# A fused attention and gated MLP kernel: casts of the next pair's q and k over three blocks, later X loads, an addition on ScalarE

## The chip, the cores and the metric

The kernel runs on one core of one Trainium2 chip. The metric is the device time of one execution in microseconds. The engines are named as the profile names them: PE (TensorE), ACT (ScalarE), DVE (VectorE), POOL (GpSimd) and SP (SyncE, which here issues DMAs).

## The reference

Attention with rotary embedding over 32 heads, its output taken as 2304 rows of 512, and a gated MLP on these rows, all in float32. `rotate` multiplies the two halves of q and k by cosines and sines of the position.

```python
def _attn_ref(q, k, v):                       # 4 x 8 heads, 576 tokens, 64 wide
    q_rot, k_rot = (rotate(q), rotate(k))
    scores = scale * np.matmul(q_rot, k_rot.transpose(0, 1, 3, 2))
    scores = scores - np.max(scores, axis=-1, keepdims=True)
    attn = np.exp(scores)
    attn = attn / (np.sum(attn, axis=-1, keepdims=True) + 1e-09)
    return np.matmul(attn, v).astype(np.float32)

def _moe_ref(x, w_gate, w_val, w_out):         # 2304 x 512, 512 x 1536 (two), 1536 x 512
    g = x @ w_gate
    silu = g * (1.0 / (1.0 + np.exp(-g)))
    val = x @ w_val
    return (silu * val @ w_out).astype(np.float32)
```

## The kernel before

**Tiling.** Attention works on 16 pairs of heads. A pair has 9 blocks of scores, 128 rows by 576 columns each; block 8 is made of the last 64 rows of both heads (its tile of exps is Et). PE works with float32 numbers that are split into a high and a low part. For each block PE writes the scores into PSUM (L349, two buffers `sc`), DVE takes the maximum (L364), ACT the exp with the sum of each row (L382), PE transposes the exps (L425, three buffers `tr`), ACT casts the transposed tile to its high part (L426) and DVE takes the low part (L427). The results are ET1 for the blocks 0 to 3 and ET2 for the rest; the columns 512 to 575 of the keys go to TK1 and TK2 (L435 to L441). PE multiplies them with the split values VS (L465, groups of ten products into one buffer `pv`), ACT copies the result to Y (L470), and SP stores it to DRAM (`yd`, L484 to L490).

**Two pairs overlap.** While pair p runs its scores, the second half of the products of pair p - 1 is still under way, and pair p + 1 is prepared. Its q and k have been loaded as X (L175) two pairs earlier and rotated on POOL one pair earlier (L206 to L208). PE transposes them in pair p in three groups: the tail (L293), q and k (L289, four transposes each). ACT casts each group to its high part into the tile N (L308), DVE adds the low part (L312). When the last group is cast, `qk_stack` issues eight DMAs on SP (L319 to L326), the folds, that lay high and low parts side by side into QK, QZ and BD, which the score products read. POOL also splits the values (L278, L279), whose load VR (L186) SP issues when the split before has ended, and prepares the MLP's operands (tiles Xab and R, L644 to L647, and weights, L724 to L731).

**What sets the order.** `PLAN` says at which block of a pair each step is written into the program. The row `qk` has three cases, for pair 0, pair 1 and all later ones; each gives the block for the groups in the order of `qkw`, which is tail, q, k for the later pairs. The program's order is kept on POOL, on PE through pair 0 and on SP through block 48 (pair 5). Elsewhere a scheduler orders the instructions of each engine anew, by its own estimates, so that an edit of `PLAN` moves neighbours as well. Each engine then works strictly in its order; SP issues a DMA only when the one before it has been issued. In pairs 3, 7, 11 and 15 `rsum` takes the reciprocal of the sums of four pairs plus 1e-9 (L392, L393), and PE transposes it in the next pair (L400). Behind attention the MLP runs with products in fewer multiplications than the plain form (L842, L1472); its first weights are loaded and cut by `wfirst` (L772), for the gate and the value, in the middle of attention and, as f = 1, in the last pair.

Of the kernel before, what the change touches and what calls it, by code (L numbers as in the profile page):

```python
# [14 lines left out]
ALU = mybir.AluOpType  # L15
# [13 lines left out]
    trb=3,  # L29
    warm=[9, 0, 1, 2, 0, 1],  # L30
    order=["qk", "scores", "trans", "pv", "exp", "evac", "rstore", "rope", "tails", "conv", "x", "conv1", "vsplit"],
    qk=[[3, 4, 6], [1, 2, 3], [0, 0, 1]],
    qkw=[[0, 2, 1], [2, 0, 1], [2, 0, 1]],
    tails=[4, 0],
    pv=[1, 6, 5, 3, 7, 8, 2, 7, 3],
    pv0=[0, 0, 0, 0, 0, 0, 10, 10, 2],
    lqk=0,
    lv=4,
    rope=1,
    vsplit=8,  # L40
# [73 lines left out]
class Attn:  # L114
# [274 lines left out]
    def rsum(self, b):  # L389
        nc = self.nc  # L390
        rt = self.rr_p.tile([128, 36], FP32, name="rt")
        nc.vector.tensor_scalar(out=rt, in0=self.sumt, scalar1=1e-9, scalar2=None, op0=ALU.add)  # L392
        nc.vector.reciprocal(out=rt, in_=rt)  # L393
        self.rt = rt

# [113 lines left out]
class Moe:  # L509
# [255 lines left out]
    def wfirst(self, f, i):  # L765
        if f == 0:
            tmp = self.again(f"xa1{'hl'[i]}", [128, 1536], U32, "raw")
        else:
            tmp = self.again(f"raw{i}", [128, (1536, 1024)[i]], U32, "raw")
        if (f, i) != (1, 1):  # L770
            self.X1 = tmp[:, 1024:1536]
        self.nc.sync.dma_start(out=tmp[:, 0:1024], in_=self.wsrc(i, f))  # L772
        raw, X = tmp[:, 0:1024].rearrange("p (f t) -> p f t", t=2), self.X1
        if f == 0:
            return self.bits10(raw, X, *self.Wb[f][i])
        return self.bits9(raw, X, *self.Wb[f][i], self.nc.gpsimd)
# [154 lines left out]
def attn_swiglu(ctx: ExitStack, tc: tile.TileContext, qk, vr, wg, wv, wo, main, tail, out):  # L931
    nc = tc.nc
# [5 lines left out]
    NP = B * H // 2  # L938
# [108 lines left out]
    P, cvq, cv1 = PLAN, {}, {}  # L1047
# [5 lines left out]
    for n in range(NB):  # L1053
        p, b = divmod(n, 9)
        if n == 9:
            ctl1.__exit__(None, None, None)
        if (p, b) == (NP - 1, 0):
            assert not any(cvq.values())
            early.close()
            moe.open_early(mctx, pl)  # L1060
        if n == 48:
            ctl0.__exit__(None, None, None)
        if n == 5:
            at.load_v(1)
        if b == (2 if 1 < p < 6 else P["lqk"]) and 0 < p < NP - 3:
            at.load_qk(p + 3)
        if b == (1 if p < 6 else P["lv"]) and 0 < p < NP - 1:
            at.load_v(p + 1)
        for name in P["order"]:
            steps[name](n, p, b)  # L1070
            if name == "qk" and n == P["qk"][0][2]:
                at.load_qk(3)
        if p == NP - 1 and ynext and NP - 2 in at.done:
            moe.yload(ynext.pop(0), 0)
# [432 lines left out]
```

## Time and profile before

| | us |
|---|---|
| time, median of 3 runs | 690.63 |
| lowest and highest of the runs | 690.6, 691.76 |
| the profiled execution, its own time | 690.11 |
| span of its profile | 688.3 |
| TensorE busy | 677.4 |
| VectorE busy | 582.4 |
| ScalarE busy | 424.2 |
| GpSimd busy | 470.1 |

The table's busy times are sums over the whole span. The granted clock of TensorE is 1.00 in all the windows read here, which is the level of 2.4 GHz. Times in a timeline are counted from the start of the span. Attention takes the time from 9.3 us, with the first scores, to 273.2 us, the last ones; a pair begins with the first score product of its block 0.

### The profile page before, as it was taken

Reading aid. Unit: us, or ns where it says so; the run is one execution under the profiler, and the core shown is the slowest. Engines: PE = TensorE matmul, PEld = TensorE weight load, DVE = VectorE, ACT = ScalarE, POOL = GpSimd, SP = SyncE. Lnnn points to the kernel's source line nnn. Section 1 sums busy time; section 2 is a strip of 40 time slices with the busy share of each in tenths; the row PEclk is TensorE's granted clock in tenths of the full one; section 3 lists DMA queues with packets and bytes.
Section 4 is the critical chain, followed back from the end, with each engine's and each line's share of the span. In section 5 each row is a group of like instructions: output and inputs, shape, how many; then the busy total and the mean of one; then the engine's idle time right before and its main releaser. Section 6 shows DMA issues by size and latency. Waiting matters only on the chain. (4 is left out here: it accounts for less than half of the span.)

```text
span 688.3 us, 12675 instructions
## 1 busy us (share of the span) xinstructions
PE 677.4 (98%) x4414; PEld 664.3 (97%) x4414; DVE 582.4 (85%) x883; ACT 424.2 (62%) x873; POOL 470.1 (68%) x475
## 2 busy tenths in 40 slices
PE   7999999999999999999999999999999999999998
PEld 6899999999999999999999999999999999999997
DVE  5888898888888888979988898988999599877683
ACT  5899988888888888555543434424435375344341
POOL 8899799999999985998889588677784720000000
PEclk9999999999999999999999999999999999999999
DMA  6897999889988879791214345354464797627101
GB/s 195 185 248 205 218 225 243 208 206 243 246 206 208 220 189 285 187 235 70 90 58 164 122 141 204 130 187 150 161 212 163 264 317 252 207 74 247 47 24 69
DMA packets 78784, 125.76 MB, mean 183 GB/s; under 512 B 16880, under 2 KB 55680, under 8 KB 78720
## 3 DMA queue, kind: packets, MB, share of 16 engines
q1 hardware_dynamic: 75248, 118.77, 60.6%
q10 hardware_dynamic: 3472, 6.18, 2.4%
q8 instruction: 35, 0.57, 0.4%
q14 instruction: 29, 0.24, 0.1%
HBM read 66.91 MB, written 33.10 MB: 145 GB/s over the span
## 5 line engine op out<-in xcount | busy, mean ns | idle before, releaser
L364 DVE TENSOR_REDUCE nmt<-sc 128x1 f32<-128x576 f32 x144 | 108.2, 751 | 20.3 <-PE sc L349 18.9
L382 ACT ACTIVATE E<-sc,nmt 128x576 f32<-128x576 f32 x128 | 97.5, 761 | 1.7 <-DVE nmt L364 1.6
L425 PE MATMUL tr<-ident,E 128*128 128x128 f32 x512 | 77.1, 274 | 0.4 <-DVE ET1l L427 0.2
L425 PEld LDWEIGHTS tr<-ident,E 128*128 128x128 f32 x512 | 61.2, 141 | 3.4 <-PE tr L289 1.3
L1472 PE MATMUL ch<-dW,dO 128*128 128x384 f32 x216 | 63.8, 337 | 0.2 <-DVE dW L1420 0.2
L206 POOL TENSOR_TENSOR t<-X,tab 128x256 f32<-128x256 f32 (+2 forms) x94 | 54.4, 600 | 9.4 <-DMA X<-in_qk_dram 5.8
L349 PE MATMUL sc<-QK 128*128 128x288 f32 x240 | 58.7, 325 | 1.4 <-ACT E L382 0.6
L426 ACT CAST ET2h<-tr 128x512 fp32r<-128x512 f32 x80 | 47.2, 590 | 14.0 <-PE tr L425 13.7
L427 DVE TENSOR_TENSOR ET2l<-tr,ET2h 128x512 fp32r<-128x512 f32 x80 | 53.1, 682 | 2.1 <-ACT ET2h L426 2.0
L349 PE MATMUL sc<-N,QZ 128*128 128x288 f32 x240 | 51.3, 296 | 0.0
L695 POOL TENSOR_TENSOR W<-WF,W 128x1024 fp32r<-128x1024 f32 x20 | 48.1, 2409 | 3.8 <-ACT W L695 3.7
L208 POOL TENSOR_TENSOR rot<-rot,t 128x512 f32<-128x512 f32 (+2 forms) x47 | 47.0, 999 | 3.7
L427 DVE TENSOR_TENSOR ET1l<-tr,ET1h 128x512 fp32r<-128x512 f32 x64 | 43.0, 685 | 7.0 <-ACT ET1h L426 6.7
L207 POOL TENSOR_TENSOR rot<-X,tab 128x512 f32<-128x512 f32 (+2 forms) x47 | 47.0, 1001 | 0.0
L1472 PE MATMUL ch<-dH,dO 128*128 128x384 f32 x156 | 45.5, 337 | 0.0
L426 ACT CAST ET1h<-tr 128x512 fp32r<-128x512 f32 x64 | 36.9, 597 | 13.1 <-PE tr L425 13.1
L842 PE MATMUL ch<-T2h,W 128*128 128x384 f32 x160 | 44.2, 337 | 0.0
L842 PE MATMUL ch<-T0h,W 128*128 128x384 f32 x160 | 44.2, 337 | 0.0
L842 PE MATMUL ch<-T1h,W 128*128 128x384 f32 x160 | 44.1, 336 | 0.0
L465 PE MATMUL pv<-ET2h,VS 128*128 128x320 f32 x128 | 40.8, 329 | 1.1 <-ACT ET2h L426 0.9
L349 PEld LDWEIGHTS sc<-QK 128*128 128x128 f32 x240 | 36.9, 190 | 4.3 <-ACT E L382 4.1
L1472 PEld LDWEIGHTS ch<-dW,dO 128*128 128x128 f32 x216 | 39.8, 188 | 0.5 <-DVE dW L1420 0.5
(349 smaller groups left out, 2300.7 us busy)
## 6 DMA issues: line engine op xcount, KB each, us to landing
QK<-N SPq DMA_DIRECT2D x64, 288.0 KB, 4.3
hd<-sg SPq DMA_DIRECT2D x14, 768.0 KB, 3.3
dB<-hd SPq DMA_DIRECT2D x8, 1152.0 KB, 7.3
X<-in_qk_dram SPq DMA_DIRECT2D x15, 576.0 KB, 5.6
yd<-Y SPq DMA_DIRECT2D x31, 256.0 KB, 5.7
raw<-in_moe_w_gate_dram SPq DMA_DIRECT2D x12, 512.0 KB, 3.7
raw<-in_moe_w_val_dram SPq DMA_DIRECT2D x12, 512.0 KB, 4.0
Xab<-yd SPq DMA_DIRECT2D x32, 192.0 KB, 4.9
```

The source lines that it names most:

```text
L206: e.tensor_tensor(out=sel(t2, u), in0=sel(x, w), in1=tb(Sn, u), op=ALU.mult)
L207: e.tensor_tensor(out=o, in0=x, in1=tb(C, slice(0, D)), op=ALU.mult)
L208: e.tensor_tensor(out=o, in0=o, in1=t2, op=ALU.add)
L349: nc.tensor.matmul(ps[:, g, 0:288], l, rr[:, o + g * 288:o + (g + 1) * 288], start=(x == 0), stop=(x == len(terms) - 1))
L364: nc.vector.tensor_reduce(out=nmcol, in_=ps[:, :, 0:288], axis=AX.XY, op=ALU.max, negate=True)
L382: nc.scalar.activation(out=E.rearrange("p (a b) -> p a b", a=2), in_=ps[:, :, 0:288], func=ACTF.Exp, bias=nmcol, scale=1.0, accum_out=self ...
L425: nc.tensor.transpose(ps[:, c], E[:, o + c * 128:o + (c + 1) * 128], self.ident)
L426: nc.scalar.copy(dst[0], src)
L427: nc.vector.tensor_tensor(out=dst[1], in0=src, in1=r32(dst[0]), op=ALU.subtract)
L695: return [lambda: self.nc.scalar.copy(h, f), lambda: le.tensor_tensor(out=l, in0=f, in1=r32(h), op=ALU.subtract)]
L842: nc.tensor.matmul(acc, l[:, w, c * 128:(c + 1) * 128], r, start=(n == 0 and k not in ONTO), stop=(n == 5), skip_group_check=True)
L1472: nc.tensor.matmul(ps, l, r[:, f], start=(new and f == 0 and x == 0), stop=(f == NFP - 1 and x == 2), skip_group_check=True)
```

## The change

Four things are edited. The row `qk` for all pairs from 2 on puts the groups tail, q, k at blocks 0, 1, 2 instead of 0, 0, 1. The load of X for pair p + 3, which stood at block 2 in pairs 2 to 5 and at block 0 in the rest, is written at block 3, behind `qk_stack` of the same pair (block 0 in pair 1, as before). The addition of 1e-9 to the sums is an ACT instruction. The raw load of `wfirst` for f = 1 is held in the program's order on SP.

```diff
@@ -29,12 +29,11 @@
     trb=3,
     warm=[9, 0, 1, 2, 0, 1],
     order=["qk", "scores", "trans", "pv", "exp", "evac", "rstore", "rope", "tails", "conv", "x", "conv1", "vsplit"],
-    qk=[[3, 4, 6], [1, 2, 3], [0, 0, 1]],
+    qk=[[3, 4, 6], [1, 2, 3], [0, 1, 2]],
     qkw=[[0, 2, 1], [2, 0, 1], [2, 0, 1]],
     tails=[4, 0],
     pv=[1, 6, 5, 3, 7, 8, 2, 7, 3],
     pv0=[0, 0, 0, 0, 0, 0, 10, 10, 2],
-    lqk=0,
     lv=4,
     rope=1,
     vsplit=8,
@@ -389,7 +388,7 @@
     def rsum(self, b):
         nc = self.nc
         rt = self.rr_p.tile([128, 36], FP32, name="rt")
-        nc.vector.tensor_scalar(out=rt, in0=self.sumt, scalar1=1e-9, scalar2=None, op0=ALU.add)
+        nc.scalar.add(rt, self.sumt, 1e-9)
         nc.vector.reciprocal(out=rt, in_=rt)
         self.rt = rt
 
@@ -769,7 +768,9 @@
             tmp = self.again(f"raw{i}", [128, (1536, 1024)[i]], U32, "raw")
         if (f, i) != (1, 1):
             self.X1 = tmp[:, 1024:1536]
-        self.nc.sync.dma_start(out=tmp[:, 0:1024], in_=self.wsrc(i, f))
+        ld = self.nc.sync.dma_start(out=tmp[:, 0:1024], in_=self.wsrc(i, f))
+        if f:
+            self.tc.keep_in_program_order(ld)
         raw, X = tmp[:, 0:1024].rearrange("p (f t) -> p f t", t=2), self.X1
         if f == 0:
             return self.bits10(raw, X, *self.Wb[f][i])
@@ -1062,7 +1063,7 @@
             ctl0.__exit__(None, None, None)
         if n == 5:
             at.load_v(1)
-        if b == (2 if 1 < p < 6 else P["lqk"]) and 0 < p < NP - 3:
+        if b == (3 if p > 1 else 0) and 0 < p < NP - 3:
             at.load_qk(p + 3)
         if b == (1 if p < 6 else P["lv"]) and 0 < p < NP - 1:
             at.load_v(p + 1)
```

The number of PE instructions is the same, and the pairs 0, 1 and 15 keep their PE order. Line numbers of the changed kernel are one lower from L38 on to about L770.

PE in pair 9, from the second block's scores on, before and after. Names: `sc` scores, `tr` transposes, `rot` the rotated q and k of pair 10, E and Et exps, `pv` products; L289 and L288 are the q and k groups.

```order
L289 MATMUL tr<-ident,rot 128x128 x4
L425 MATMUL tr<-ident,Et 128x128 x4
L349 MATMUL sc<-QK_92 128x288 x2
L349 MATMUL sc<-N_91,QZ_94 128x288 x2
L435 MATMUL tr<-ident,E 128x128 x2
L437 MATMUL tr<-ident,Et 128x2x64
L349 MATMUL sc<-QK_92 128x288 x2
L349 MATMUL sc<-N_91,QZ_94 128x288 x2
L289 MATMUL tr<-ident,rot 128x128 x4
L465 MATMUL pv<-ET2h,VS_141 128x320
L425 MATMUL tr<-ident,E 128x128 x4
```

```order
L424 MATMUL tr<-ident,Et 128x128 x4
L348 MATMUL sc<-QK_92 128x288 x2
L348 MATMUL sc<-N_91,QZ_94 128x288 x2
L434 MATMUL tr<-ident,E 128x128 x2
L436 MATMUL tr<-ident,Et 128x2x64
L464 MATMUL pv<-ET2h,VS_141 128x320
L288 MATMUL tr<-ident,rot 128x128 x4
L348 MATMUL sc<-QK_92 128x288 x2
L348 MATMUL sc<-N_91,QZ_94 128x288 x2
L424 MATMUL tr<-ident,E 128x128 x4
L464 MATMUL pv<-ET2l,VS_141 128x320
```

The q group stood first of these rows and the k group ahead of the first ET2 product; now the first ET2 product stands ahead of the q group, and the k group comes ten rows behind the last one shown, after the scores of block 4.

ACT in pair 9, from the exp of block 0 on, before and after. N is the tile of q and k, Y a copy of a result, `128x4x2x64` the ET2 cast of block 8.

```order
L382 ACTIVATE E,sumt<-sc,nmt 128x576
L470 COPY Y_2460<-pv 128x256
L308 CAST N_91<-tr 128x512
L382 ACTIVATE E,sumt<-sc,nmt 128x576
L426 CAST ET2h<-tr 128x4x2x64
L440 CAST TK2h<-tr 128x384
L382 ACTIVATE E,sumt<-sc,nmt 128x576
L308 CAST N_91<-tr 128x512
```

```order
L381 ACTIVATE E,sumt<-sc,nmt 128x576
L469 COPY Y_2460<-pv 128x256
L307 CAST N_91<-tr 128x3x64
L425 CAST ET2h<-tr 128x4x2x64
L381 ACTIVATE E,sumt<-sc,nmt 128x576
L439 CAST TK2h<-tr 128x384
L381 ACTIVATE E,sumt<-sc,nmt 128x576
L307 CAST N_91<-tr 128x512
```

The ET2 cast of block 8 stood behind the exp of block 1 and stands ahead of it; the q cast (`128x512`) stood ahead of that exp and stands behind the exp of block 2; the tail cast (`128x3x64`) has come in from the pair before.

ACT in pair 3, from the tail cast to the k cast, the second `128x512`, before and after.

```order
L308 CAST N_91<-tr 128x3x64
L385 COPY Et<-Et 128x64
L724 ACTIVATE raw<-raw 128x512
L382 ACTIVATE E,sumt<-sc,nmt 128x576
L470 COPY Y_913<-pv 128x256
L308 CAST N_91<-tr 128x512
L382 ACTIVATE E,sumt<-sc,nmt 128x576
L426 CAST ET2h<-tr 128x4x2x64
L440 CAST TK2h<-tr 128x384
L382 ACTIVATE E,sumt<-sc,nmt 128x576
L308 CAST N_91<-tr 128x512
```

```order
L307 CAST N_91<-tr 128x3x64
L381 ACTIVATE E,sumt<-sc,nmt 128x576
L425 CAST ET2h<-tr 128x4x2x64
L381 ACTIVATE E,sumt<-sc,nmt 128x576
L439 CAST TK2h<-tr 128x384
L307 CAST N_91<-tr 128x512
L381 ACTIVATE E,sumt<-sc,nmt 128x576
L425 CAST ET1h<-tr 128x4x128
L381 ACTIVATE E,sumt<-sc,nmt 128x576
L307 CAST N_91<-tr 128x512
```

Between the tail cast and the k cast there were three exps and no ET1 cast; now there are four exps and an ET1 cast, while the two copies and the raw step have gone ahead of these rows.

SP in pair 2, at the end of the folds, before and after. X is the load for pair 5, `raw` one of the MLP's weights.

```order
L324 DMA QZ_114<-N_111 64x512
L325 DMA BD_113<-N_111 64x2x64
L326 DMA BD_113<-N_111 64x2x64
L175 DMA X<-in_qk_dram 128x1152
L772 DMA raw<-in_moe_w_val_dram 128x1024
L489 DMA yd_57<-Y_786 128x2x256
L490 DMA yd_57<-Y_786 128x2x64
```

```order
L323 DMA QZ_114<-N_111 64x512
L324 DMA BD_113<-N_111 64x2x64
L325 DMA BD_113<-N_111 64x2x64
L771 DMA raw<-in_moe_w_val_dram 128x1024
L174 DMA X<-in_qk_dram 128x1152
L488 DMA yd_57<-Y_779 128x2x256
L489 DMA yd_57<-Y_779 128x2x64
```

The X load stood directly behind the folds, ahead of the raw load, and stands behind both. In pairs 3 and 4 it stands directly behind the folds in both versions.

## Rows read from the trace of the kernel before

**Rows 1.** The page: busy us of each engine, share of the span, instructions.

```profile
PE 677.4 (98%) x4414; PEld 664.3 (97%) x4414; DVE 582.4 (85%) x883; ACT 424.2 (62%) x873; POOL 470.1 (68%) x475
```

**Rows 2.** Windows (length; PE PEld DVE ACT POOL busy; clock; DMA share; GB/s): pairs 3, 5, 9.

```profile
59.22:76.01 16.79, 16.40 (x132) 15.97 (x131) 15.35 (x26) 15.51 (x39) 15.66 (x17) 1.00 0.82 210
...
93.54:110.57 17.03, 16.80 (x133) 15.90 (x131) 15.66 (x27) 15.49 (x40) 16.39 (x19) 1.00 0.93 222
...
160.13:176.59 16.46, 16.36 (x132) 15.95 (x131) 14.39 (x24) 14.57 (x37) 15.66 (x19) 1.00 0.99 250
600.00:650.00 50.00, 50.00 (x288) 50.00 (x287) 34.70 (x33) 22.31 (x26) 0.00 (x0) 1.00 0.38 127
```

**Rows 3.** Timeline, TensorE weight loads, pair 9: start us, duration us, [idle <-releaser].

```profile
165.13 0.30 PEld L349 LDWEIGHTS sc<-QK 128*128 128x128 f32 x2 [0.34 <-ACT E L382]
...
166.45 0.31 PEld L425 LDWEIGHTS tr<-ident,E 128*128 128x128 f32 x3 [0.17 <-PE tr L289]
```

**Rows 4.** Timeline, ScalarE and then VectorE, pair 9.

```profile
163.76 0.59 ACT L308 CAST N<-tr 128x512 fp32r<-128x512 f32 x1 [0.19 <-PE tr L289]
164.24 0.75 ACT L382 ACTIVATE E<-sc,nmt 128x576 f32<-128x576 f32 x1
...
164.97 0.59 ACT L426 CAST ET2h<-tr 128x512 fp32r<-128x512 f32 x1
...
165.65 0.68 DVE L427 TENSOR_TENSOR ET2l<-tr,ET2h 128x512 fp32r<-128x512 f32 x1
```

**Rows 5.** Timeline, matmuls of TensorE, pair 9.

```profile
160.13 0.51 PE L349 MATMUL sc<-QK 128*128 128x288 f32 x2
160.47 0.43 PE L349 MATMUL sc<-N,QZ 128*128 128x288 f32 x2
...
162.59 0.43 PE L349 MATMUL sc<-QK 128*128 128x288 f32 x2
162.85 0.44 PE L349 MATMUL sc<-N,QZ 128*128 128x288 f32 x2
163.12 0.60 PE L289 MATMUL tr<-ident,rot 128*128 128x128 f32 x4
163.56 0.60 PE L425 MATMUL tr<-ident,Et 128*128 128x128 f32 x4
163.91 0.52 PE L349 MATMUL sc<-QK 128*128 128x288 f32 x2
...
166.86 0.39 PE L465 MATMUL pv<-ET2l,VS 128*128 128x320 f32 x1
167.09 0.31 PE L465 MATMUL pv<-ET2h,VS 128*128 128x320 f32 x1
```

**Rows 6.** Timeline, TensorE, pair 4.

```profile
81.58 0.41 PE L465 MATMUL pv<-ET2h,VS 128*128 128x320 f32 x1 [0.88 <-ACT ET2h L426]
```

**Rows 7.** Timeline, ScalarE, pair 3: the k cast.

```profile
65.86 0.65 ACT L308 CAST N<-tr 128x512 fp32r<-128x512 f32 x1
```

**Rows 8.** Timeline, SyncE and then GpSimd, pairs 3 and 4.

```profile
66.54 0.61 SPq L319 DMA_DIRECT2D QK<-N  x1
...
74.46 0.59 SPq L175 DMA_DIRECT2D X<-in_qk_dram  x1
...
80.12 0.60 POOL L206 TENSOR_TENSOR t<-X,tab 128x64 f32<-128x64 f32 x2 [3.76 <-DMA X<-in_qk_dram]
```

**Rows 9.** Timeline, GpSimd, pair 9: end of the split of V.

```profile
162.52 1.57 POOL L279 TENSOR_TENSOR VS<-VR,VS 128x640 fp32r<-128x640 f32 x1
```

**Rows 10.** Timeline, SyncE, pair 9: V load and last fold.

```profile
164.68 0.54 SPq L186 DMA_DIRECT2D VR<-in_vr_dram  x1
...
172.48 1.07 SPq L323 DMA_DIRECT2D QK<-N  x1
```

**Rows 11.** Source view of L323, ten pairs from 100 to 258 us.

```profile
DMA to landing us min/median/max: 4.7/5.4/7.1
```

**Rows 12.** Timeline, TensorE, pair 10: scores of block 1.

```profile
179.05 0.43 PE L349 MATMUL sc<-QK 128*128 128x288 f32 x2
```

## The prediction

> **What bounds the kernel now.** The page's busy line comes first: TensorE is busy 98% of the span, VectorE 85%, the others less [rows 1]. So time can only go where TensorE waits or works slowly, and the table of windows shows where: an undisturbed pair of heads takes 16.46 us (pair 9), pair 3 takes 0.33 more and pair 5 0.57 more, and pair 4 has one wait of 0.88 us ahead of its first ET2 product [rows 2, 6]. Behind attention TensorE has no gap to give or take (50.00 of 50.00 us) [rows 2], so I let a lead won in attention reach the end. Inside a steady pair TensorE waits in two places [rows 3]: 0.34 us ahead of the score group of block 3, for the exp of block 1 that frees its PSUM buffer (I call this group S3), and 0.17 us ahead of the transposes of block 0 (T0), for a transpose buffer that VectorE's low part of the last ET2 cast frees (165.65 + 0.68 = 166.33) [rows 4].
>
> GpSimd is the second clock. It waits 3.76 us for X(6) and starts at 80.12 [rows 8]; from there its work follows without such a wait to the end of the ropes, 15.7 of 16.46 us busy in pair 9 [rows 2]. SyncE issues in order: in pair 9 the V load waits for GpSimd's split, which ends at 162.52 + 1.57 = 164.09, and all eight folds into QK stand behind it, the last one issued at 172.48 [rows 9, 10]. Folds of that line land 4.7 to 7.1 us after their issue, 5.4 in the median [rows 11], so this one at about 177.9. The first scores that read it, block 1 of pair 10, start at 179.05 [rows 12]. So TensorE can gain 179.05 - 177.88 = 1.17 us on GpSimd's clock (no more, and by the ends of the landing times 0 to 1.87) before these folds hold it. This room is the crux of the sum.
>
> **The change, part by part.** Sums are made on the profiled execution, 690.11 us, which lies 0.52 under the median of the runs, 690.63; I carry the difference over to the median.
>
> *Casts over blocks 0, 1, 2, steady pairs.* No instruction is added; the q transposes and their cast go behind the first ET2 product, the k ones behind the next score group. ScalarE had in pair 9: exp of block 0, Y copy, an idle 0.19, q cast 0.48 from start to start, exp of block 1 at 164.24 [rows 4]. Now the idle goes, the 192-wide tail cast (taken as 0.21, from less than half the 512 columns that took 0.48) comes in, and an ET2 cast of the same 512 columns takes the place of the q cast. So the exp ends as before, within 0.02, and S3 may start as before, but TensorE has one 320-column product more behind it by then, 0.23 us with the gap behind a transpose (166.86 to 167.09) [rows 5]. S3's wait falls from 0.34 to 0.10. The ET2 cast now precedes that exp instead of following it (164.97 before), so its low part frees T0's buffer some 0.7 to 0.8 earlier; T0 itself is reached nearly as much earlier, and its wait falls from 0.17 to 0.13. The product that is pulled ahead waits for this cast: about 0.12, a new wait. That is 0.35 instead of the 0.51 of the rows, a gain of 0.16; the same addition made for the old order gives 0.60, so against itself it gains 0.25. I take **-0.25 a pair**, since an addition is best compared with the same addition; bounds -0.51 (both waits gone) and +0.10 (the addition's own error of about 0.1, with no gain).
>
> *More places where transposes turn to products.* The new order has 206 of them, the old 189. The second half of a score group takes 0.34 behind a transpose (160.13 to 160.47), 0.26 behind a product (162.59 to 162.85) [rows 5]. If the 0.08 belonged to the turn, 17 x 0.08 = +1.4 us. But a transpose group followed by another takes 0.44 (163.12 to 163.56) and one followed by scores 0.35 (163.56 to 163.91) [rows 5]: the 0.08 is paid in both cases, once per group, and the groups are as many. I take 0 and keep 1.4 as a bound.
>
> *The same in the early pairs, 2 to 5.* There the excess is 0.33 + 0.88 + 0.57 = 1.78 us [rows 2, 6]. The two score groups that stood side by side in pair 3 are apart now, and in pair 4 a score group comes between the transposes of the sums and the product that waited 0.88. I take the two thirds of it that are those places, 0.33 + 0.88 = **-1.2**; bounds -1.78 and +0.51 (the two steady waits once more).
>
> *Loads behind the folds.* In pair 3 the first fold is issued at 66.54, with the end of ScalarE's k cast (65.86 + 0.65), and eight folds later, at 74.46, X(6); it lands as GpSimd starts, at 80.12 [rows 7, 8]. In the new order ScalarE does one exp (0.73) and one 512-column cast (0.48) more between the pair's first exp and that k cast [rows 4], 1.21 us; less some 0.3 that TensorE has won by then, the folds and X(6) come **0.9 us later**, and GpSimd's clock with them. Bounds: 0, and one whole block, 16.46 / 9 = 1.83. X(5) goes behind one raw load too; it makes rope(5) late, which the 3.76 us ahead of rope(6) cover [rows 8]. From pair 6 on the X load moves by three blocks of nine, and the next pair's rope is the first to read it: no cost; were that cover gone, GpSimd's clock would be late and the price that of the folds of pair 10, below.
>
> *The addition on ScalarE.* Four instructions of 128x36, one per four pairs. On ScalarE each costs at most what a 512-column cast costs, 0.48 [rows 4], in pairs where it idles 16.46 - 14.57 = 1.9 us [rows 2]; VectorE gives up as small a piece, and its reciprocal waits for the other engine now; behind it stand the maxima of the next blocks. 0, bounds -0.2 and +0.2 (half a cast). *Raw weight loads of the last pair in order*: the same loads, one or two places away on SyncE behind Xab loads: 0, within the same bounds.
>
> **The sum.** TensorE's lead as pair 10 begins would be 1.2 + 4 x 0.25 = 2.2 us. The folds of pair 10 allow 1.17 - 0.9 = 0.27. So 0.3 of the lead survives, and pairs 10 to 14 add 5 x 0.25 = 1.25, because GpSimd, 15.7 busy per 16.46 us pair, is faster than TensorE and the room opens again. -0.27 - 1.25 = **-1.5 us**: 688.6 on the profiled basis, **689.1 us** on the median.
>
> A fold of 288 KB lands 5.4 us after its issue [rows 11]. The Trainium skill, page "DMA: Bandwidth & Descriptors", section "Anatomy of one DMA — SWDGE (gpsimd) path", fits a DMA as about 2.0 us plus its bytes at 436 GB/s, so some 2.7 us here by estimate; that fit is for another issuing path, and the trace does not agree. By it the room would be 2.7 us larger and the folds would hold nobody, the time of the first rival.
>
> **The rivals.**
> *The folds do not hold TensorE.* It needs X(6) on time (lower bound 0 instead of 0.9) and the folds of pair 9 landing about 1 us sooner, as they may when the four R loads ahead of them have drained (the last fold is issued 172.48 - 164.68 = 7.8 us behind the V load, though nine issues of about 0.6 would take 5.4 [rows 10]). Then the whole lead stays: 1.2 + 9 x 0.25 = 3.45, 687.2 us. Against it: in-order issue, and the windows' DMA share of 0.99 in pair 9 [rows 2].
> *GpSimd's clock is a whole block late, and steady pairs win only the 0.16 of the rows.* The folds of pair 10 then cost 1.83 - 1.17 = 0.66, five pairs give back 0.8: -0.14, 690.5 us, no change. For it: ScalarE is the engine that orders the k cast in pair 3, and works there without a pause. That the order changes nothing that is waited for comes out here as well.
> *Slower: the q and k casts hold the exps.* The k cast and a Y copy now stand between the exps of blocks 3 and 4, where block 6 of the scores waits for the latter. The price of a cast that stands in TensorE's way is on record: 0.88 us in pair 4 [rows 6]. At 0.88 a pair: 9 x (0.88 - 0.25) - 1.2 = +4.5, 695.1 us; it decides (over 692.0) from 9 x (s - 0.25) - 1.2 = 1.4, s = 0.54 a pair. Against it: my addition finds 1.6 us of room at that group and 1.0 at the one before. For it: VectorE is 14.4 and ScalarE 14.6 of 16.46 us busy in the pair [rows 2], so queues that are once late do not soon recover.
>
> **How the numbers follow.** Forecast 0.42, folds hold nobody 0.22, GpSimd late 0.20, slower 0.16. A measurement of this kernel can tell some 0.2% from no change, 1.4 us: faster is under 689.25, slower over 692.0. The forecast's own spread (early pairs by 0.6, GpSimd's clock by 0.9, a steady pair by 0.1) puts it over that bound in somewhat under half of its cases. Faster 0.42 x 0.55 + 0.22 = 0.45; slower 0.16; the rest, 0.39, the same. The range goes from the first rival less 0.4 for the early pairs' bound, 686.8, to 691.8, which takes in the second rival and the turns' 1.4; what is left out is the slow rival and little else.
>
> **What would show it.** Right: a steady pair (6 to 8) of 16.2 us with the wait ahead of S3 near 0.1; rope(6) starting about 0.9 later than 80.12 with a wait for X; and in pair 10 a wait ahead of the scores of block 1 that a DMA of the folds ends, some 1.5 to 2 us long, then pairs of 16.2. First rival: no such wait. Second: rope(6) near 82 and pairs near 16.3. Third: pairs above 16.5, TensorE waiting for an exp in blocks 4 to 7. What would make it wrong: a lead that is lost again behind attention, where GpSimd's preparation of the MLP's operands may be waited for, or other leads of the early pairs than I guess.

## The result and the profile after

The changed kernel takes **697.81 us** (median of four runs, 697.22 to 698.47) beside 690.82 for the kernel before in the same comparison: ratio 1.0099, interval 1.0081 to 1.0116. It is 7.0 us slower where 1.5 us less were forecast, and outside the range. The profiled execution, the longest of the four, took 698.47 us, 8.36 more than the one of before (690.11).

The page's busy line and six windows of the kernel after (columns as in [rows 2]): pairs 3, 5, 6, 9, 10 and the stretch behind attention.

```profile
PE 679.0 (97%) x4414; PEld 666.3 (96%) x4414; DVE 581.9 (84%) x879; ACT 427.5 (61%) x877; POOL 469.8 (67%) x475
```

```profile
61.30:77.03 15.73, 15.07 (x122) 14.67 (x120) 13.95 (x24) 14.84 (x38) 10.07 (x13) 1.00 0.86 219
95.05:115.51 20.46, 17.07 (x132) 15.90 (x131) 16.95 (x27) 17.27 (x43) 19.20 (x22) 1.00 0.87 228
115.51:133.36 17.85, 17.85 (x130) 17.49 (x130) 13.33 (x22) 13.38 (x34) 17.12 (x20) 0.90 0.82 188
166.16:183.88 17.72, 16.46 (x133) 16.01 (x131) 15.30 (x25) 16.12 (x41) 16.92 (x23) 1.00 1.00 235
183.88:200.07 16.19, 16.19 (x130) 15.94 (x130) 13.24 (x22) 13.35 (x35) 15.39 (x20) 1.00 0.87 214
600.00:650.00 50.00, 50.00 (x287) 50.00 (x287) 36.06 (x36) 21.12 (x25) 0.00 (x0) 1.00 0.49 162
```

Busy lines hardly differ from [rows 1]; the windows tell the places. Pair 10 is what was hoped for, 16.19 instead of 16.46. Pair 5 has 3.43 us more than in [rows 2], pair 6 runs at a granted clock of 0.90, pair 9 ends in a wait. Pair 3 is 1.06 shorter, but a group of ten products has moved from it into pair 2 (17.07, before 15.53), so pairs 2 to 5 must be taken as one sum: 71.28 us, before 66.88.

TensorE's matmuls that began behind a wait, in the timeline of the kernel after:

```profile
64.26 0.40 PE L348 MATMUL sc<-QK 128*128 128x288 f32 x1 [0.66 <-ACT E L381]
...
82.23 0.41 PE L464 MATMUL pv<-ET2h,VS 128*128 128x320 f32 x1 [0.72 <-ACT ET2h L425]
...
93.23 0.40 PE L348 MATMUL sc<-N,BD 128*128 128x288 f32 x1 [0.46 <-ACT E L381]
...
99.92 0.33 PE L434 MATMUL tr<-ident,E 128*128 128x128 f32 x1 [1.14 <-DVE ET2l L426]
...
115.51 0.71 PE L348 MATMUL sc<-QK 128*128 128x288 f32 x2 [2.19 <-DMA QK<-N]
...
183.88 0.37 PE L348 MATMUL sc<-QK 128*128 128x288 f32 x1 [1.26 <-DMA QK<-N]
...
279.81 0.40 PE L348 MATMUL sc<-QK 128*128 128x288 f32 x1 [0.85 <-ACT E L381]
```

In pairs 3 to 5 ScalarE and VectorE are waited for four times, 2.98 us in all. The kernel before has three waits there, 1.49 us: the 0.88 of [rows 6] and two for exps, in the timeline of its TensorE:

```profile
64.50 0.40 PE L349 MATMUL sc<-QK 128*128 128x288 f32 x1 [0.39 <-ACT E L382]
...
97.48 0.40 PE L349 MATMUL sc<-QK 128*128 128x288 f32 x1 [0.22 <-ACT E L382]
```

Two long waits are for folds: 2.19 at the first scores of pair 6 and 1.26 at the first of pair 10 (a third, of 0.38, is ahead of pair 14). The last is in pair 15.

Added up between the two profiled executions, from the starts of the pairs: up to pair 2 +0.54 (start-up, where no cause shows; other kernels here have up to 0.9), pairs 2 to 5 +4.40, pair 6 +1.39, pairs 7 to 14 +0.43 (the wait of 1.26 against the gain of the steady pairs), from pair 15 on +1.60: 8.36.

**Why the folds of pair 6 came late.** SyncE and, in the last two lines, ScalarE's k cast and GpSimd in pair 5 of the kernel after (three timelines); the X load at 107.87 is that of pair 9.

```profile
97.98 0.59 SPq L174 DMA_DIRECT2D X<-in_qk_dram  x1
...
99.68 0.78 SPq L185 DMA_DIRECT2D VR<-in_vr_dram  x1
107.87 0.35 SPq L174 DMA_DIRECT2D X<-in_qk_dram  x1
108.31 0.62 SPq L318 DMA_DIRECT2D QK<-N  x1
...
104.88 0.57 ACT L307 CAST N<-tr 128x512 fp32r<-128x512 f32 x1
...
106.55 1.30 POOL L206 TENSOR_TENSOR rot<-X,tab 128x512 f32<-128x512 f32 x1
```

And SyncE of the kernel before, the same pair:

```profile
101.22 0.62 SPq L319 DMA_DIRECT2D QK<-N  x1
...
109.20 0.58 SPq L175 DMA_DIRECT2D X<-in_qk_dram  x1
...
110.88 0.49 SPq L175 DMA_DIRECT2D X<-in_qk_dram  x1
```

SyncE's program order is kept only up to block 48, which is block 3 of pair 5. The changed kernel writes the loads X(8) and X(9) behind that point, and the scheduler pulled both ahead of the folds of pair 5. X(8) found its buffer free. X(9) takes the buffer of X(7), which GpSimd reads last at 106.55 + 1.30 = 107.85: SyncE stood idle from 100.46 to 107.87, and all eight folds stood behind. They had no need to go before 105.45, when the k cast ended (104.88 + 0.57); so X(9) held them up for some 2.9 of these 7.41 us. The wait shows on no line of TensorE's own, only as "DMA QK". The Trainium skill, page "DMA: Bandwidth & Descriptors", section "Anatomy of one DMA — SWDGE (gpsimd) path" (written for DMAs that GpSimd issues), says that any wait for a semaphore happens on the issuing sequencer before dispatch, not in the DMA engines; these rows agree, with 7.41 us of idle sequencer.

**The clock behind the wait.** Windows of one us of the kernel after, around the start of pair 6 (columns as in [rows 2]):

```profile
114.00:115.00 1.00, 0.00 (x0) 0.00 (x0) 0.28 (x1) 0.67 (x2) 1.00 (x1) 1.00 1.13 226
115.00:116.00 1.00, 0.49 (x2) 0.42 (x3) 0.00 (x0) 0.00 (x0) 1.00 (x2) 0.82 0.99 214
116.00:117.00 1.00, 1.00 (x5) 0.98 (x5) 0.14 (x1) 0.00 (x0) 1.00 (x2) 0.50 0.98 198
...
118.00:119.00 1.00, 1.00 (x7) 1.00 (x7) 0.88 (x2) 1.00 (x4) 0.92 (x4) 0.50 0.93 259
119.00:120.00 1.00, 1.00 (x10) 1.00 (x10) 0.03 (x1) 0.61 (x4) 0.92 (x2) 0.98 0.64 151
```

TensorE idles for 2.19 us, and then the granted clock is 0.50 for over 3 us, the level of 1.2 GHz; 5 to 7 matmuls start in a microsecond instead of 10. Pair 6 takes 17.85 us, 1.66 more than pair 10; the mean clock of 0.90 gives nearly the same, 17.85 x 0.10 = 1.8 us, by estimate.

### The profile page after: what moved, and what is told of

Read it like the earlier page. It is cut to its first block, busy times and chain, and to the rows that moved or that the text cites. A ratio compares the mean times of both kernels' runs of the same rounds, so it can differ in the third digit from the quotient of the medians.

```text
span 696.7 us, 12753 instructions
## 1 busy us (share of the span) xinstructions
PE 679.0 (97%) x4414; PEld 666.3 (96%) x4414; DVE 581.9 (84%) x879; ACT 427.5 (61%) x877; POOL 469.8 (67%) x475
## 4 chain that ended last, share of the span: by engine, by line
PE 75%; DMA 8%; DVE 6%; POOL 4%; ACT 3%; issue 2%; SPq 1%; ACTq 0%; DVEq 0%; POOLq 0%
PE ch L843 27%; PE ch L1473 14%; PE sc L348 10%; PE pv L464 10%; PE tr L424 7%; PE ch L795 4%; DMA QK<-N 4%; POOL Z L700 2%; PE tr L288 2%; DVE dB L1411 1%; DMA yd<-Y 1%; DVE dO L1392 1%; DMA dO<-od 1%; PE tr L434 1%; DMA od<-FOf 1%
```

## The experiments

Times are medians, ratios against the kernel before on the same chip (its medians lay between 690.66 and 690.86). A diff is against the changed kernel where nothing else is said. "Pairs 2 to 5" and the like are sums of pair lengths in the profiled executions.

**One part alone.** First the new `qk` row in the kernel before, then the new place of X in it, then the addition.

```diff
-    qk=[[3, 4, 6], [1, 2, 3], [0, 0, 1]],
+    qk=[[3, 4, 6], [1, 2, 3], [0, 1, 2]],
```

> The kernel before with the casts over blocks 0, 1, 2 alone; X loads, the addition and the raw loads as before. PE's order is nearly that of the changed kernel; on SyncE the X loads of pairs 2 to 5 now stand ahead of the folds, and in pair 5 both X(8) and X(9) do. Theory A (X(9) blocks the queue): as slow in pairs 5 and 6 as the changed kernel, but no late rope(5) and rope(6): 694 to 697 us, with a wait of 2 us or more for a fold as pair 6 starts. Theory B (it is the loads behind the folds that cost, by way of GpSimd's clock): 688 to 690.5 us, no such wait.

Measured: 695.71 us, ratio 1.0065 (1.0041 to 1.0089). The casts alone are slower, but not in the way that theory A told: there is no wait for a fold as pair 6 starts, so that the time fell into its range by luck. X(9) does stand ahead of the folds of pair 5 here; but the ropes are earlier, GpSimd reads X(7) for the last time at 102.54, X(9) is issued at 102.56, and the first fold goes at 106.24 with the end of its k cast (106.22). So the casts alone put X(9) ahead of the folds, and only with the later ropes that the later X loads bring (last read at 107.85) does it hold them.

Pairs 2 to 5 take 69.24 (+2.4), the steady pairs 16.2, and pair 14 ends in a wait of 3.51. TensorE and SyncE in this kernel:

```profile
94.16 0.40 PE L349 MATMUL sc<-N,BD 128*128 128x288 f32 x1 [1.19 <-ACT E L382]
...
265.07 0.50 PE L349 MATMUL sc<-QK 128*128 128x288 f32 x2 [3.51 <-DMA QK<-N]
...
253.95 1.52 SPq L772 DMA_DIRECT2D raw<-in_moe_w_val_dram  x1
...
256.28 0.62 SPq L320 DMA_DIRECT2D QK<-N  x1
```

The raw loads of the last pair have come between the folds of pair 15. A fold of L320 lands in 4.3 us in the median, the one issued at 256.28 in 8.7. These two loads are the ones that the fourth part holds in order, and this run is without it; in the changed kernel, with X(9) held and with late casts they stand behind the folds. How much of the 3.51 us is the lack of that part, no run tells.

```diff
-        if b == (2 if 1 < p < 6 else P["lqk"]) and 0 < p < NP - 3:
+        if b == (3 if p > 1 else 0) and 0 < p < NP - 3:
```

> The kernel before with the X loads behind the folds alone; casts, addition and raw loads as before. The other engines keep their order almost as before; on SyncE X(5) goes behind a raw load, X(8) ahead of the V load of pair 5, and X(9) stays behind the folds. Theory A: X(9) does not block, X(5) is late by about half a us, so 690.8 within 1 us. Theory B (loads behind the folds cost by themselves): 692.5 or more, rope(6) starting 1 us or more later than 80.1.

Measured: 691.0 us, 0.9998 (0.9986 to 1.001). The new place costs nothing with the old casts: the folds come early enough to stay ahead of X(9). So the 4 us of the next experiment belong to the two parts together: the casts move the folds behind X(9), the later X loads make X(9) wait.

```diff
-        nc.vector.tensor_scalar(out=rt, in0=self.sumt, scalar1=1e-9, scalar2=None, op0=ALU.add)
+        nc.scalar.add(rt, self.sumt, 1e-9)
```

> The kernel before with the addition of 1e-9 on ScalarE alone. SyncE and GpSimd keep their order; the others differ in some ten rows each around the four additions. Every theory: no difference that can be measured, 690.8 within 0.7 us; the pair behind a reciprocal stays at 16.64 us.

Measured: 690.8 us, 1.0001 (0.9991 to 1.001). The addition costs nothing that can be measured. The fourth part, the held raw loads, was not run by itself, so its price is not shown.

**The X load that waits.** X(9) alone is kept in SyncE's program order.

```diff
-            sy(out=X, in_=self.qk[p])
+            ld = sy(out=X, in_=self.qk[p])
+            if p == 9:
+                self.tc.keep_in_program_order(ld)
```

> The changed kernel with X(9) alone held in the program's order, which puts it among the folds for pair 7 instead of ahead of those for pair 6; every other engine in the same order. Theory A2: the 2.19 us wait ahead of pair 6 and the half clock behind it go; pairs 2 to 5 still 1 us longer than before, the waits ahead of pair 10 and in pair 15 stay: 693 to 695.5 us. Rival (the wait moves on to another pair in full): 696.5 or more.

Measured: 693.4 us, 1.0041 (1.0026 to 1.0055), 2.7 us over the kernel before instead of 7.0: some 4 us go with the place of this one load. The first fold of pair 5 is issued 10.25 us behind the start of the pair (104.42) instead of 13.26, pair 5 takes 17.85, and the clock stays at 1.00. Against the expectation no fold is waited for at pair 10 either. What is left against before: pairs 2 to 5 +1.12, pair 6 +0.33, pairs 7 to 14 -1.57, from pair 15 on +2.54. There TensorE waits for an exp in the last pair, behind a step of the weights' preparation on VectorE. The profile puts that step's wait down to GpSimd; the raw load that it reads, issued at 262.91, landed 7.8 us later at the earliest, at 270.7, so that it may have been the load. TensorE and VectorE:

```profile
273.70 0.40 PE L350 MATMUL sc<-QK 128*128 128x288 f32 x1 [1.28 <-ACT E L383]
...
270.83 1.28 DVE L752 TENSOR_SCALAR raw<-raw 128x512 uint32<-128x512 uint32 x1 [1.47 <-POOL xm L693]
```

All X loads from X(8) on held (`if p > 7:` in the diff above):

> The changed kernel with one edit: the X loads for pairs 8 and up are held in the order of the program, so that on SyncE X(9) no longer stands ahead of the folds for pair 6. PE, ACT, DVE and POOL keep their order; only SyncE's differs. Theory A (SyncE's queue: X(9) waits until rope(7) has read the last of the buffer that it takes, and the folds behind it wait with it): the first fold for pair 6 is issued near 104 us instead of 108.3, the 2.19 us wait ahead of pair 6 and the longer first block of pair 6 go, and the time falls by 3.5 to 5 us, to about 693.5. Theory B (the folds are late because the k cast itself, or GpSimd's clock, is late): the folds wait for their casts all the same, the time stays within 1 us of 697.8.

Measured: 697.01 us, 1.0083 (1.0054 to 1.0113), which by the time alone would speak for theory B. The wait ahead of pair 6 is gone, as theory A has it, but X now stands among the folds of pair 8 and delays them. (The execution of this trace took 694.8 us, the least of four; the others took up to 699.01.) SyncE, then TensorE:

```profile
135.33 0.58 SPq L174 DMA_DIRECT2D X<-in_qk_dram  x1
...
138.19 0.61 SPq L321 DMA_DIRECT2D QK<-N  x1
...
146.92 0.49 PE L350 MATMUL sc<-QK 128*128 128x288 f32 x2 [2.04 <-DMA QK<-N]
```

That fold took 8.6 us to land (its line's median is 4.4), with a load of 576 KB issued 2.9 us ahead of it. The same with X back at block 2 in pairs 2 to 5 and at block 0 in the later ones, as before (`2 if 1 < p < 6 else 0`):

> The changed kernel with the X loads of pairs 2 to 5 back at block 2 (which, with the new casts, is ahead of the folds), and those from X(8) on held in the program's order. So no X load waits for the folds, and X(9) does not stand ahead of those for pair 6. Theory A with its second part (late X(5) and X(6) put GpSimd's clock 2.5 us late, which costs the 1.3 us wait ahead of pair 10 and a part of what pairs 2 to 4 lose): rope(6) no later than 80.1, pairs of 16.2 us, no long wait ahead of pair 6 or 10, 688 to 690.5 us. If the new order of casts loses time by itself in pairs 2 to 5: 691 to 693.5 us, with exps waited for there.

Measured: 695.18 us, 1.0073 (1.005 to 1.0096), above both ranges. Pairs 2 to 5 take 69.55, with the later X (the experiment before) 67.89. So the later X is not what makes them long: beside the new casts it saves some 1.5 us there, and the casts alone are the worse for lacking it.

**Which pairs lose.** New casts only from pair 6 on, X at block 2 in pairs 2 to 5:

```diff
-        w, bs = P["qkw"][min(p, 2)], P["qk"][min(p, 2)]
+        w, bs = P["qkw"][min(p, 2)], P["qk"][min(p, 2)] if p < 2 or p > 5 else [0, 0, 1]
-        if b == (3 if p > 1 else 0) and 0 < p < NP - 3:
+        if b == (2 if 1 < p < 6 else 3 if p > 1 else 0) and 0 < p < NP - 3:
```

> The changed kernel with the casts over blocks 0, 1, 2 only from pair 6 on; pairs 2 to 5 have them at 0, 0, 1 and their X loads at block 2, as before. So X(9) is behind the folds for pair 6 and rope(6) as early as before. Theory A2 (the gain of 0.27 us a pair is real; the loss is that of the early pairs and of SyncE's order there): pairs 6 to 14 of 16.2 us, pairs 2 to 5 as before, and at most the wait for a fold ahead of pair 15, whose folds have a raw load between them: 688.5 to 690 us. Rival (the folds come too late wherever the casts spread over three blocks): waits for folds of 1 us or more ahead of several pairs, 691 or more.

Measured: 690.89 us, 1.0001 (0.9992 to 1.001), above the range of theory A2 and without the many waits of the rival. Pairs 2 to 5 take 66.51, pairs 6 to 13 130.60 instead of 132.05. As pair 14 begins TensorE is 1.37 us ahead of before by the clock of the trace, and then it gives it back. SyncE and TensorE:

```profile
249.98 0.59 SPq L781 DMA_DIRECT2D raw<-in_moe_w_gate_dram  x1
...
252.29 0.59 SPq L319 DMA_DIRECT2D QK<-N  x1
...
259.57 0.50 PE L348 MATMUL sc<-QK 128*128 128x288 f32 x2 [1.88 <-DMA QK<-N]
```

New casts only in pairs 2 to 5, with X(9) as in the changed kernel (`if p < 6 else [0, 0, 1]`):

> The changed kernel with the casts over blocks 0, 1, 2 only in pairs 2 to 5, and 0, 0, 1 from pair 6 on; X loads as in the changed kernel, with X(9) ahead of the folds for pair 6. Theory A2: pairs 2 to 6 together as much longer than before as in the changed kernel (about 4.4 us, and 1.4 in pair 6 at half the clock), the later pairs 16.46 us, no wait ahead of pair 10 since TensorE is late itself: 695 to 697 us. Rival: the early pairs alone do not cost more than 1.5 us, under 692.5.

Measured: 694.76 us, 1.0062 (1.0046 to 1.0077), just under the range. The loss of the early part is here and no gain of the late one, but not all of it: pairs 2 to 6 are 4.4 us longer than before, in the changed kernel 5.8, and the granted clock stays at 1.00. Pairs 3 and 4 take 15.73 and 18.02, to the hundredth what they take in the changed kernel, and X(9) stands again ahead of the folds, with 1.74 us of wait at 114.32.

**Would a fixed order of SyncE heal it?** The idea was that every loss comes from the scheduler's freedom. SyncE was kept in program order to the end of attention: in the changed kernel, in the one with late casts, and in the kernel before (the line that holds the raw loads drops out of the first two).

```diff
-        if n == 48:
-            ctl0.__exit__(None, None, None)
...
+    ctl0.__exit__(None, None, None)
```

> The changed kernel, all four parts, with SyncE kept in the program's order to the end of attention; PE and POOL keep the changed kernel's order word for word, ACT and DVE but for ten rows at the end. So in each pair the eight folds are issued first, then X, then the V load. Theory A3 (the time is lost in SyncE's queue: behind X(9) in pair 5, behind the V load that waits for GpSimd in pairs 9 and 14, behind Xab and raw loads in pairs 14 and 15): no wait for a fold of 1 us or more, steady pairs of 16.2 us, pairs 2 to 5 about 1 us longer than before in sum: 688.5 to 691.5 us. Rival (TensorE's new order is late by itself, the queue only shows it): 693.5 or more.

> The kernel with the casts over blocks 0, 1, 2 from pair 6 on (as in the run of late casts), with SyncE in the program's order to the end of attention. Theory A3: the lead of some 2 us that TensorE had there as pair 15 began is not lost to the wait for the folds (1.88 us): 688 to 689.5 us. Rival (the folds of pair 15 come late because GpSimd or the DMA queues are late, wherever they stand on SyncE): the wait stays, 690.3 us or more.

> The kernel before with SyncE in the program's order to the end of attention, the casts at 0, 0, 1; PE and POOL keep the order of before word for word. It separates the two: if the order on SyncE alone made the gain, this would be as fast as the run of late casts in this order, under 689.5. By theory A3 TensorE waits for no fold before, so nothing is gained: 690 to 691.5 us, pairs of 16.46 us.

Measured: 705.68 us (1.0212), 704.16 (1.0196), 701.38 (1.0149). The idea fell. From pair 15 on the three take 8.7, 10.1 and 9.2 us more than the kernel before: the written order issues the raw gate load 12.0, 12.3 and 13.8 us behind the start of that pair, where the kernel before does so 1.8 us behind it, and VectorE's step on it waits. So most of what they lost lies behind the start of the last pair, and the three runs do not single out the folds. With late casts TensorE waits, among other places, here:

```profile
179.20 0.37 PE L348 MATMUL sc<-QK 128*128 128x288 f32 x1 [2.61 <-DMA QK<-N]
...
287.37 0.47 PE L424 MATMUL tr<-ident,E 128*128 128x128 f32 x1 [4.05 <-ACT E L381]
```

**The last pair.** X(9) held, and the steps of the last weight's preparation (`c1`) one block later:

```diff
-    c1=[[3, 3, 4, 4, 5, 5, 6, 6, 6], [7]],
+    c1=[[4, 4, 5, 5, 6, 6, 7, 7, 7], [7]],
```

> The run with X(9) held, with the weight steps of the last pair (ACT, DVE, POOL work on the raw gate load) one block later in the program, at blocks 4 to 7 instead of 3 to 6; SyncE's order is unchanged. Theory C (in pair 15 VectorE stands 1.5 us at such a step, which waits for GpSimd and the raw load, and the maxima, exps and scores behind it wait with it): the 1.28 us wait of TensorE in pair 15 goes, the time falls by 1.2 to 2 us, to 691.5 to 692.3. Rival (pair 15 is late for the folds or Y stores and the step only stands where the time is lost): within 0.7 us of 693.4.

Measured: 696.37 us, 1.0081 (1.0068 to 1.0094), 3.0 worse than without it, against both expectations. The wait of 1.28 is gone, a larger one has come, and behind it the granted clock is 0.50 for 3 us. SyncE, ScalarE and TensorE:

```profile
272.38 4.52 SPq L638 DMA_DIRECT2D Xab<-yd  x3
276.99 0.55 SPq L490 DMA_DIRECT2D yd<-Y  x1
...
278.77 0.37 ACT L471 COPY Y<-pv 128x256 f32<-128x256 f32 x1 [4.50 <-DMA yd<-Y]
...
279.20 0.58 PE L466 MATMUL pv<-ET1h,VS 128*128 128x256 f32 x1 [4.20 <-ACT Y L471]
```

The store that frees the Y tile stood behind Xab loads. SyncE's order is the same in this run and in the one with X(9) held, so the order alone does not make this loss: with the step out of the way TensorE met the next thing that the queue held back. Late casts were then ended earlier, so that the end of attention is ordered differently: first with pair 14 on the old row (`5 < p < 14`), then with pairs 13 and 14 on it (`5 < p < 13`, so pairs 6 to 12 have the new one); all else is as with late casts.

> The run of late casts, with the casts over blocks 0, 1, 2 in pairs 6 to 13 only; pair 14 has them at 0, 0, 1, so that the k cast ahead of pair 15's folds is about 1.9 us earlier in the pair, and no raw load stands among these folds. Theory D (the 1.88 us wait ahead of pair 15 is made there, by the late k cast and the raw load ahead of the folds): the wait falls under 0.7 us and the time to 688.7 to 689.8 us. Rival E (SyncE's queue and the DMA load, which keep GpSimd's clock, land these folds at the same time whatever TensorE has won, as in the kernel before): a wait of 1.5 us or more stays, 690.2 to 691.2 us.

> The same in pairs 6 to 12 only; SyncE's order from pair 14 on is then that of the kernel before word for word. Theory D: a lead of 7 x 0.25 less what the turn into the new order costs, about 1.2 to 1.7 us, is kept to the end: 689 to 689.8 us. Rival E: it is lost ahead of pair 15, in a wait for a fold that the kernel before does not show: 690.3 to 691.2 us.

Measured: 694.09 us (1.0047, 1.0031 to 1.0064) and **689.46 us** (0.9986, 0.9975 to 0.9997). In the first the wait for folds is gone, as theory D has it, but its time is missed: SyncE's order in the last pairs is again a new one, VectorE waits 4.25 us for the raw gate load in pair 15, TensorE 3.58 us for an exp, and behind that the granted clock is 0.50 for 3 us. In the second that order is the one of before, and no long wait comes:

```profile
273.14 0.81 DVE L750 TENSOR_SCALAR raw<-raw 128x512 uint32<-128x512 uint32 x1 [4.25 <-DMA raw<-in_moe_w_gate_dram]
...
275.54 0.40 PE L348 MATMUL sc<-QK 128*128 128x288 f32 x1 [3.58 <-ACT E L381]
```

```profile
192.45:208.66 16.21, 16.21 (x132) 15.96 (x131) 14.22 (x24) 14.69 (x38) 15.40 (x20) 1.00 0.85 210
```

(VectorE and TensorE in the first kernel; pair 11 of the second, columns as in [rows 2].) This version beats both kernels, by 1.3 us against before by the medians; its interval, 0.2 to 1.7 us, only just excludes no change. From pair 2 to pair 15 its profiled execution takes 213.59 us, before 215.39.

## Why the prediction was wrong

*Steady pairs, -0.25: right.* Undisturbed pairs take 16.18 to 16.22 after, 16.46 before, also where only these casts are changed. The pairs 8 and 12, each behind a reciprocal, gain less: 16.58, before 16.64. How the gain is made up was not right: in pairs 7 and 10 of the kernel after no weight load shows a wait within the pair, where [rows 3] have 0.34 and 0.17 and I had left 0.10, 0.13 and 0.12. The 0.51 is gone, and the pair is only about half of that shorter; so that -0.25 came out is in part luck.

*"From pair 6 on the X load moves by three blocks of nine ...: no cost": this step failed*, and it is the largest loss. I counted by blocks in the program, though the order of SyncE is the scheduler's from block 48 on. X(9), the first load that waits for a buffer behind that point, went ahead of eight folds. Holding it alone gives back some 4 us of 7.0. The prediction saw the cover gone only on GpSimd's side, as a late rope; the folds that the load could pass on SyncE were not looked at. It took two parts of the change that were priced apart: the later casts, with which X(9) comes ahead of the folds also by themselves (casts alone), and the later ropes, which keep its buffer until 107.85 instead of 102.54.

*Early pairs, -1.2: wrong in sign, and outside its upper bound of +0.51.* With X(9) held they cost +1.12, with the casts alone +2.4; with the old casts there (late casts) 66.51, -0.4. That these casts are the cause is shown; by what way is not. The waits for E at 64.26 and 93.23 are in blocks 2 and 8, not in blocks 4 to 7 as the third rival had it, and no steady pair has them. Just ahead of these exps ScalarE has no q or k cast, but a cast of exps, and in pair 3 the tail cast behind it, where VectorE had the maximum ready at 62.79:

```profile
62.68 0.58 ACT L425 CAST ET2h<-tr 128x512 fp32r<-128x512 f32 x1
63.15 0.33 ACT L307 CAST N<-tr 128x192 fp32r<-128x192 f32 x1
63.35 0.77 ACT L381 ACTIVATE E<-sc,nmt 128x576 f32<-128x576 f32 x1
```

I took two places to be cured because their neighbours changed, with no row for the queues of ScalarE and VectorE behind them, which [rows 2] show fuller there (15.51 and 15.35 of 16.79 us in pair 3) than in pair 9 (14.57 and 14.39 of 16.46).

*GpSimd's clock 0.9 us later: mis-sized.* rope(5) and rope(6) in the timeline of GpSimd after:

```profile
67.05 0.60 POOL L205 TENSOR_TENSOR t<-X,tab 128x64 f32<-128x64 f32 x2 [5.26 <-DMA X<-in_qk_dram]
...
82.54 0.32 POOL L205 TENSOR_TENSOR t<-X,tab 128x64 f32<-128x64 f32 x1 [0.92 <-DMA X<-in_qk_dram]
```

rope(6) starts 2.4 us later than in [rows 8]; the lead of 0.3 that I had subtracted was a delay: pair 3 begins at 61.30, before 59.22, of which 0.54 is start-up and the rest is pair 2, longer by the ten products.

*The crux, a wait for a fold at pair 10: there, 1.26 us, but not as told.* GpSimd's split ended at 166.61 (before 164.09, [rows 9]) and the V load was issued only at 172.34, so GpSimd did not hold the folds. SyncE's queue did: the k cast ended at 175.19 and the first fold into QK was issued only at 176.58, behind four other folds, in a pair whose DMA share is 1.00. With X(9) held, or with late casts, the wait is absent, though there TensorE comes to pair 10 earlier (177.87 and 176.05, here 183.88). The room of 1.17 us was therefore no bound. What makes the queue of pair 9 late in the changed kernel alone I did not test further.

*"A lead won in attention reaches the end": wrong.* With late casts 1.37 us of lead at pair 14 became a wait of 1.88 at pair 15. Behind attention [rows 2] were right (50.00 of 50.00 in both), but the last two pairs come ahead of it, and there SyncE has weights, Xab loads, Y stores and folds in one queue. With X(9) held this costs 2.54 us, in the changed kernel 1.60. The waits ahead of pair 15 with casts alone and with late casts go with raw loads between the folds; in the changed kernel it is the raw load's own landing. The kernel before issues that load at 260.90 (first line), 1.8 us behind the start of pair 15, the changed kernel 4.2 us behind it, as the timelines of SyncE, VectorE and ScalarE show:

```profile
260.90 0.57 SPq L772 DMA_DIRECT2D raw<-in_moe_w_gate_dram  x1
...
270.05 0.54 SPq L771 DMA_DIRECT2D raw<-in_moe_w_gate_dram  x1
...
277.79 0.43 DVE L750 TENSOR_SCALAR raw<-raw 128x512 uint32<-128x512 uint32 x1 [1.90 <-DMA raw<-in_moe_w_gate_dram]
...
278.92 0.74 ACT L381 ACTIVATE E<-sc,nmt 128x576 f32<-128x576 f32 x1 [1.31 <-DVE nmt L363]
```

The load is issued at 270.05, VectorE's step on it waits 1.90, the maximum behind it and the exp come late, and TensorE waits 0.85 at 279.81. Over the runs VectorE comes to this step the later the later the load is issued, both counted from the start of pair 15: at 10.0 us for a load at 1.3 to 2.0 (before, casts in pairs 6 to 12 and three others), 10.7 for 2.3 (late casts), 10.8 to 11.5 for 3.6 to 3.8 (the three runs with X held), 12.0 for 4.2 (the changed kernel), 14.5 for 6.4 (casts in pairs 6 to 13), 20.4 for 13.8 (the kernel before with SyncE in program order). That the place of this load is the whole of the loss from pair 15 on is argued from these chains; no run moved it alone.

*The addition: 0, right* (1.0001; it lasts 0.25 us on ScalarE). *The held raw loads and the turns between transposes and products, 0 as well, are not tested.* The held loads were not run apart. The turns were not measured apart either; their bound of 1.4 is 0.1 a pair, and steady pairs that lost 0.51 of waits and only 0.27 of their time leave room for it.

The slow rival gave 695.1 with a loss in every pair. The time went past it, but not by its way: no steady pair lost, and the waits for exps came in other blocks than it named. That it lay nearest is luck.

## What to carry to other kernels

Where a scheduler orders a queue, ask of every load that an edit moves past the point where the order is held which buffer it takes, when that is last read, and what stands behind it in the queue; a load that waits for its buffer makes everything behind it wait. Judge an edit of a steady loop in its start and end as well, where the queues are fuller: here the same casts win 0.25 us in a steady pair, lose in the first four and disturb the last two. And two parts that are harmless or small apart can meet: a load that had passed the folds did no harm until another part made its buffer late. Confining the edit to the pairs where it wins turned +7.0 us into -1.3, with an interval from -1.7 to -0.2.

## What the runs showed of the hardware

A wait of TensorE can cost more than its length: behind 2.19 us of idling at 113.3 to 115.5 the granted clock was 0.50 in the windows from 116 to 119, and behind 3.51 us with the casts alone it was 0.50 in those from 266 to 269; behind 3.58 us (casts in pairs 6 to 13) it was 0.50 from 276 to 279. Behind 1.26 us at pair 10, 1.74 with early casts and 1.88 with late casts it stayed at 1.00, and behind 2.04 us with all X loads held the mean clock of that execution is 1.000; in the other three executions of that kernel it was 0.995 to 0.997. So a wait's length alone does not tell, and the same kernel may pay this in one execution and not in the next. The Trainium skill, page "TensorE: Matmul & The Clock Gate", section "Part 1: The HAM clock gate", tells of a gate that passes half of the clock's pulses; the 0.50 agrees. I had priced waits of up to 2 us at their length alone.

Folds of one line and size land in very different times: L320 (casts alone) in 4.0 to 8.7 us, L321 (X held) in 4.0 to 8.6, the longest ones close behind a load of X or of raw weights on the same queue. With late casts that of L319 behind a raw load took 7.1, its line 4.3 in the median. [rows 11] gave 7.1 as the longest, and I had used the median.
